# First layers of batches three and four: the seven-product block method applied a second time in four of the products, with weight sums kept in memory

## The chip, the cores and the metric

The kernel runs on one core of one Trainium2 chip. The metric is the device time of one execution in microseconds. In this text PE is TensorE (matrix products), DVE is VectorE, ACT is ScalarE, POOL is GpSimd and SP is SyncE, whose queue issues nearly all DMAs here. Every engine works through its own list of instructions in order and waits on semaphores for the others.

## What is computed

Attention with a mask by cluster (queries and keys see each other where their nearest centroids agree), for 4 batches, 8 heads, 768 positions and head size 64, and on its output a feed-forward block:

```python
attn = softmax(where(mask, q @ k.T / 8, -1e9)) @ v      # (4, 8, 768, 64)
x = attn.transpose(0, 2, 1, 3).reshape(3072, 512)
h = x @ w_in                                            # 512 x 2048
g = h * (1.0 / (1.0 + np.exp(-1.702 * h)))
out = g @ w_out                                         # 2048 x 512
```

All of it is fp32. Only the feed-forward block, and in it the first product with w_in, is touched by the change.

## The kernel before

**Stages.** First the attention of all four batches runs (to about 400 us); x of batch 0 stays on the chip, x of the later ones is kept in DRAM (`kept`) and loaded before its batch. Then the four batches of the feed-forward block follow, b = 0 to 3: a first layer (`first7` in batch 0, `first7_psum` later) and a second layer (`second49`, called for k = 0 to 6).

**Block method.** Both layers use Winograd's form of Strassen's method: a product of 2 x 2 blocks by 7 products instead of 8, with sums of blocks before and after. The first layer uses it once. The output is features by tokens; the 2048 features are two rows of FB = 8 blocks of 128, the 768 tokens two halves of HALF = 384, the inner dimension 512 two columns of two chunks of 128. For each f of 8, the seven products give G[:, f] and G[:, f+8], each with two halves h. One product has 2 matmuls of the program (c = 0, 1), 128 x 128 weights and 384 columns of x, so a first layer has 8 x 14 = 112; the profile shows two records for each matmul. The second layer uses the method twice: seven outer products (k, in the order 1, 2, 3, 6, 5, 7, 4), each of seven inner ones with 4 matmuls of QT = 192 columns, so 196 matmuls.

**Sums of weights, first layer.** `sums_w` makes for each block f the sums S2, S1, S4 on POOL, two blocks ahead, into pool `wq` (2 buffers); in batch 0 also S3, written over its place in w_in and kept there.

**Sums of x.** `sums_x` makes on DVE the tiles T2, T3, T4 (with T1 in place of an x tile) in the last steps of the second layer before.

**`first7_psum`** runs per f the products in the order 1 and 7 (w_in blocks), S2, S1, S3, S4, and w_in's (1,1). Three PSUM banks of the pool `ps_b` (6 banks) are used per f; a bank is accumulated into again after ACT (`nc.scalar.copy`) or DVE (`add`) has read it. ACT ends each quarter of G with gelu (`finish`). `after7(f)` makes on DVE one difference of G's quarters and, for f of 4 and more, the four sums `sums_t(0, f - 4)` that the second layer's k = 0 will need (M6, M5, M7, M4 there).

**`second49(k)`** runs its inner products in the order 1, 2, 6, 5, 7, 3, 4. The first goes to bank x and is copied by ACT (y11, L951); the third (6) accumulates into x. Products 6, 5 and 3 need sums of w_out's blocks (`W`, tile Wz, three thirds of 256 KB, two buffers), loaded from `kept_w` by `load_sums(k + 2)`, which SP issues after the second49 that frees the buffer. Through `extra`, the second layer's own sums, the output stores and the sums of x are spread between DVE's other work. The weights of k = 2, 3, 4 are Z_of[4], Z_of[2], Z_of[1], sums of w_out made once in batch 0; they stay on the chip. The results go to Y tiles (sums on POOL, or on DVE in the first and last batch for two of them).

**What sets the order.** Nothing is reordered by a planner (`manual_schedule`): the order on each engine is that in which the program issues its instructions. After each first layer SP has the eight loads of x for the next batch; output stores of a batch are issued at k = 4 (one of four) and in the next first layer (three, `do(pend, 1)`, one per f).

## Time and profile before

| what | value |
|---|---|
| median of 3 executions | 895.45 us (894.76 to 896.04) |
| the profiled execution | 895.92 us |
| its span, first to last instruction | 894.1 us |
| PE busy | 883.0 us (99%) |
| DVE, ACT, POOL busy | 678.4, 385.6, 482.0 us |
| a first layer of batches 1 to 3 on PE | 72.24 us |
| a second layer on PE | 63.77 us |
| DVE busy in batch 1's first layer (478.5 to 550.75 us) | 27.75 us |
| DVE busy in batch 1's second layer (550.75 to 614.5 us) | 58.03 us |
| DMA moved in all | 78.98 MB |

Times within the span count from its first instruction. A line of the timeline gives start, length, engine, source line, operation, output from inputs with their shapes, and the number of merged instructions; in brackets is the idle time before it and what ended it. A line number can be that of a helper (L598 is every sum of `sums`, L845 every `add`). A line of the table of stretches gives from:to, length, busy time and number of instructions for each engine, the granted clock of PE, the busy share of the DMA engines and GB/s.

### The profile page before, as it was taken

What the parts mean: (1) busy time and instruction counts of PE and PEld (TensorE: products, weight loads), DVE (VectorE), ACT (ScalarE), POOL (GpSimd) and SP (SyncE); (2) the same over time, 40 slices, a digit from 0 to 9 for tenths busy, and PEclk for the clock granted to TensorE, in tenths of its full rate; (3) what the DMA queues carried; (4) which work ended last, traced back from release to release, by engine and by line L of the source; (5) the groups of instructions that cost most, each with busy time, mean ns of one, the idle gap of its engine ahead of it and who ended that gap; (6) DMA issues with size and microseconds to landing.
All of it is one profiled execution on the core that took longest, in us unless ns stands there. A gap on an engine that the chain in (4) does not pass through costs nothing.

```text
span 894.1 us, 17678 instructions
## 1 busy us (share of the span) xinstructions
PE 883.0 (99%) x6720; PEld 581.9 (65%) x6720; DVE 678.4 (76%) x1097; ACT 385.6 (43%) x867; POOL 482.0 (54%) x459
## 2 busy tenths in 40 slices
PE   8999999999999999999999999999999999999997
PEld 3444444444454445557997557997556998556996
DVE  3999989999889997998896335796335797325795
ACT  3577776777677774322112333112333112333111
POOL 5899999998999998694220222233232133220130
PEclk9999999999999999999999999999999999999999
DMA  9576566666665210026213102322202223200224
GB/s 176 117 132 115 104 120 123 151 132 138 133 140 127 86 44 19 0 107 229 89 60 119 35 1 71 104 68 102 46 1 71 83 66 118 53 1 0 72 72 110
DMA packets 176334, 78.98 MB, mean 88 GB/s; under 512 B 152824, under 2 KB 159472, under 8 KB 176240
## 3 DMA queue, kind: packets, MB, share of 16 engines
q1 hardware_dynamic: 175984, 77.63, 35.8%
q8 instruction: 55, 0.90, 0.4%
q14 instruction: 39, 0.32, 0.1%
q10 hardware_dynamic: 256, 0.13, 0.1%
HBM read 61.03 MB, written 16.70 MB: 87 GB/s over the span
## 4 chain that ended last, share of the span: by engine, by line
PE 94%; DVE 4%; issue 1%; DMA 1%; ACT 0%; SPq 0%; ACTq 0%; DVEq 0%
PE b L941 25%; PE b L889 24%; PE s L472 14%; PE o L537 14%; PE b L854 8%; PE s L495 3%; PE m L554 3%; DVE G L598 2%; PE m L348 1%; DVE E L598 1%; DMA in<-in_k_dram 1%; DVE Tx L598 0%; PE o L296 0%; DVE G L845 0%; DVE y L845 0%
## 5 line engine op out<-in xcount | busy, mean ns | idle before, releaser
L521 POOL TENSOR_TENSOR sum<-sum,A 128x384 f32<-128x384 f32 x252 | 266.0, 1092 | 24.9 <-ACT A L503 16.4
L503 ACT ACTIVATE A<-s 128x768 f32<-128x768 f32 x192 | 146.1, 808 | 90.5 <-PE s L495 71.6
L845 DVE TENSOR_TENSOR G<-b,G 128x384 f32<-128x384 f32 x128 | 69.5, 556 | 142.0 <-PE b L889 135.7
L598 POOL TENSOR_TENSOR Y<-y,Y 128x768 f32<-128x768 f32 x24 | 58.1, 2435 | 165.8 <-DVE y L845 141.9
L472 PE MATMUL s<-T,T 64*64 64x384 f32 x1536 | 143.0, 487 | 0.7 <-ACT A L503 0.7
L537 PE MATMUL o<-A,inv 64*64 64x384 f32 x1536 | 141.4, 483 | 0.0
L598 POOL TENSOR_TENSOR W<-w_in 128x256 f32<-128x256 f32 x32 | 23.6, 736 | 184.8 <-PE b L889 175.0
L598 DVE TENSOR_TENSOR G<-G 128x768 f32<-128x768 f32 (+1 forms) x92 | 105.5, 1171 | 0.0
L472 PEld LDWEIGHTS s<-T,T 64*64 64x64 f32 x1536 | 55.1, 132 | 69.9 <-ACT A L503 36.4
L537 PEld LDWEIGHTS o<-A,inv 64*64 64x64 f32 x1536 | 58.9, 133 | 38.0 <-issue 32.8
L889 PE MATMUL b<-x,W 128*128 128x384 f32 x192 | 69.8, 486 | 0.0
L889 PE MATMUL b<-Tx,w_in 128*128 128x384 f32 x192 | 69.8, 486 | 0.0
L889 PE MATMUL b<-x,w_in 128*128 128x384 f32 x192 | 65.8, 486 | 0.0
L897 ACT ACTIVATE G<-G 128x384 f32<-128x384 f32 x72 | 37.7, 524 | 52.1 <-DVE G L845 52.1
L941 PE MATMUL b<-G,w_out 128*128 128x192 f32 x320 | 55.9, 326 | 0.0
L941 PEld LDWEIGHTS b<-G,w_out 128*128 128x128 f32 x320 | 52.7, 190 | 1.1
L889 PEld LDWEIGHTS b<-x,W 128*128 128x128 f32 x192 | 36.5, 190 | 25.4
L889 PEld LDWEIGHTS b<-Tx,w_in 128*128 128x128 f32 x192 | 36.5, 190 | 25.4
L889 PEld LDWEIGHTS b<-x,w_in 128*128 128x128 f32 x192 | 36.4, 190 | 24.6
L941 PE MATMUL b<-E,Wz 128*128 128x192 f32 x288 | 50.5, 327 | 0.1
L941 PEld LDWEIGHTS b<-E,Wz 128*128 128x128 f32 x288 | 47.3, 190 | 0.6 <-DVE E L598 0.4
L495 PE MATMUL s<-rows,rows 64*64 64x384 bf16 x720 | 45.6, 323 | 0.0
(182 smaller groups left out, 1518.2 us busy)
## 6 DMA issues: line engine op xcount, KB each, us to landing
Wz<-kept_w SPq DMA_DIRECT2D x78, 256.0 KB
raw<-in_moe_w_in_dram SPq DMA_DIRECT2D x16, 512.0 KB
raw<-in_moe_w_out_dram SPq DMA_DIRECT2D x16, 512.0 KB
inv<-in_v_dram SPq DMA_DIRECT2D x16, 384.0 KB
in<-in_q_dram SPq DMA_DIRECT2D x60, 96.0 KB
in<-in_k_dram SPq DMA_DIRECT2D x60, 96.0 KB
kept<-x SPq DMA_DIRECT2D x24, 192.0 KB
x<-kept SPq DMA_DIRECT2D x24, 192.0 KB
```

The source lines that it names most:

```text
L472: nc.tensor.matmul(out=ps[c:c + D, a, 0:HALF], lhsT=T[p, 1][rows, kt * P + c:kt * P + c + D], rhs=T[p, 0][rows, h * HALF:(h + 1) * HALF], ...
L495: nc.tensor.matmul(out=s_of[u][c:c + D, a, :], lhsT=rows_of[1, p % 2][rows, kt * P + c:kt * P + c + D], rhs=rows_of[0, p % 2][rows, h * HA ...
L503: nc.scalar.activation(out=A_of[u], in_=s_of.pop(u), func=AF.Exp, scale=SCALE)
L521: nc.gpsimd.tensor_tensor(out=sum_of[g][:, a], in0=(A_of[u - 1] if kt == 1 else sum_of[g])[:, a], in1=A_of[u][:, a], op=ALU.add)
L537: nc.tensor.matmul(out=o_of[g][a * D:(a + 1) * D, r, 0:HALF], lhsT=v_in[p][rows, a, kt, :], rhs=A[rows, a, :], start=(kt == 0), stop=(kt = ...
L554: nc.tensor.matmul(out=ps[a * D:(a + 1) * D, 0:HALF], lhsT=twos, rhs=sm[:, a, :], start=(i == 0), stop=(i == len(parts) - 1))
L598: engine.tensor_tensor(out=o, in0=a, in1=b, op=(ALU.add if op == "+" else ALU.subtract))
L845: nc.vector.tensor_tensor(out=o, in0=p, in1=a, op=ALU.add)
L854: nc.tensor.matmul(out=ps[:, 0:HALF], lhsT=a[:, c], rhs=x(c), start=(c == 0), stop=(c == 1))
L889: nc.tensor.matmul(out=ps, lhsT=a[:, c], rhs=x(c), start=start and c == 0, stop=(c == 1), skip_group_check=True)
L897: nc.scalar.activation(out=g, in_=g if ps is None else ps, func=AF.Gelu_apprx_sigmoid, scale=2.0)
L941: nc.tensor.matmul(out=ps, lhsT=A[n][:, f], rhs=M[n][:, f], start=start and f == 0, stop=(f == FQ - 1), skip_group_check=True)
```

## The change

- **Batch 0.** After the first layer the three Z tiles are also written to DRAM (`kept_z`, 3 x 1 MB), and after every later first layer they are loaded back, because batches 1 to 3 use their place for first-layer weights in the meantime. The POOL sums of batch 1's first two blocks are made after k = 4 of the second layer (`sums_w1`), no longer in the first layer.
- **Batch 1.** The first layer takes its blocks in the order 0, 4, 1, 5, 2, 6, 3, 7. When a pair (j, j + 4) is done, `inner_w` makes on DVE eight sums of 256 columns, the sums of weights that the second application of the method needs, and SP stores 1.5 MB to DRAM (`kept_i`).
- **Batches 2 and 3.** `first49` replaces the eight calls of `first7_psum`, and no first-layer sums are made on POOL. It works on four pairs j. Products 1, 6 and 7 (`whole`) stay as they were, 384 columns wide, in the two banks of `ps_m`; the other four are each done by seven inner products (`inner`) of 192 columns: 28 matmuls of the program per j in six banks of `ps_b`. Its 16 sums of x are made on DVE at its start. Results are put together by ACT copies, `add` from PSUM, and sums in place (`add_y5`, `close`); gelu takes a quarter of G for both blocks of a pair (768 columns). The weights of a pair are loaded from `kept_i` (`load_inner`): those of j = 0 and 1 after k = 4 of the second layer before, the later ones inside.

The diff, cut to its core:

```diff
...
     kept_w = spill.tile([7, 3, P, FQ, P], FP32, name="kept_w")
+    kept_z = spill.tile([3, P, FB, DN], FP32, name="kept_z")
+    kept_i = spill.tile([FQ, P, 24, P], FP32, name="kept_i")
+    tq = acc_p.tile([P, 2, QT], FP32, name="tq")
+    Zb = {i: z.rearrange("p f (x n) -> p (f x) n", n=P)
+          for i, z in Z_of.items()}
     def Bz(row, col, f):
...
+    TURN = [f + m * FQ for f in range(FQ) for m in range(2)]
+    def sums_w1(n):
+        if n >= FB:
+            return
+        f = TURN[n]
+        S = Zb[1 + n // 2 % 2][:, n % 2 * 6:n % 2 * 6 + 6].rearrange(
+            "p (i c) n -> p i c n", c=2)
+        w_of[FB + f] = {1: S[:, 0], 2: S[:, 1], 3: A_in(1, 0, f), 4: S[:, 2],
+                        0: S}
+        S = w_of[FB + f]
+        A11, A12, A22 = A_in(0, 0, f), A_in(0, 1, f), A_in(1, 1, f)
+        sums(nc.gpsimd, ((S[2], A22, "-", S[3]), (S[1], S[2], "+", A11),
+                         (S[4], A12, "-", S[2])))
+    def inner_w(j, S):
+        st = Zb[4]
+        def of_s(m, c):
+            return S[m][:, 0:3:2, c]
+        def of_w(m, c):
+            at = (j + m * FQ) * P
+            return w_in[:, 2 + c, :].rearrange("p (r x) -> p r x", r=2)[
+                :, :, at:at + P]
+        for n, (a, s3) in enumerate(((of_s, st[:, 0:2]),
+                                     (of_w, of_w(1, 0)))):
+            s2, s1, s4 = (st[:, i:i + 2] for i in range(2 + 6 * n, 8 + 6 * n, 2))
+            sums(nc.vector, ((s3, a(0, 0), "-", a(1, 0)),
+                             (s2, a(1, 1), "-", s3),
+                             (s1, s2, "+", a(0, 0)),
+                             (s4, a(0, 1), "-", s2)))
+        for at, x in ((slice(0, 14), st[:, 0:14]),
+                      (slice(14, 20), S[0].rearrange("p i c n -> p (i c) n")),
+                      (slice(20, 22), S[1][:, 1]),
+                      (slice(22, 24), S[1][:, 0:3:2, 1])):
+            nc.sync.dma_start(out=kept_i[j, :, at], in_=x)
+    def load_inner(j, parts=(0, 1)):
+        if j < FQ:
+            for n in parts:
+                o = (Zb[1 + j % 2], Zb[4][:, j % 2 * 8:j % 2 * 8 + 8])[n]
+                nc.sync.dma_start(
+                    out=o, in_=kept_i[j, :, (slice(0, 16), slice(16, 24))[n]])
+    Gq = G.rearrange("p f h (q t) -> p (f h q) t", t=QT)
+    SETS = ((2, 5), (3, 4))
+    def first49(X, T):
+        b = {o: {(c, q): x[:, q * QT:(q + 1) * QT]
+                 for c in range(2) for q in range(2)
+                 for x in ((X[1, 0, c], T[1, c], X[1, 1, c], T[4, c])[n],)}
+             for n, o in enumerate((2, 5, 3, 4))}
...
+        M = {}
+        for o in b:
+            M[o] = {1: b[o][0, 0], 2: b[o][1, 0], 3: b[o][1, 1],
+                    7: b[o][0, 1], **{n: rooms.pop(0) for n in (6, 5, 4)}}
+        for todo in ((2, 5), (3, 4)):
+            for n, one, op, two in ((7, 3, "-", 7), (6, 7, "+", 1),
+                                    (5, 3, "-", 6)):
+                for o in todo:
+                    sums(nc.vector, ((M[o][n], M[o][one], op, M[o][two]),))
+        for o in b:
+            sums(nc.vector, ((M[o][4], M[o][2], "-", M[o][6]),))
...
+        def quarter(j, r, h):
+            at = r * FB + j
+            return G[:, at:at + FQ + 1:FQ, h]
+        def halves(ps):
+            return ps[:, 0:HALF].rearrange("p (o t) -> p o t", t=QT)
+        def gelu(j, r, h):
+            g = quarter(j, r, h)
+            nc.scalar.activation(out=g, in_=g, func=AF.Gelu_apprx_sigmoid,
+                                 scale=2.0)
+        def whole(j, n):
+            if n == 1:
+                whole_of[j] = bank(), bank()
+            for m in range(2):
+                f = j + m * FQ
+                at = j % 2 * 8 + m * 4
+                a = {1: A_in(0, 0, f), 6: Zb[4][:, at:at + 2],
+                     7: A_in(1, 0, f)}[n]
+                x = {1: lambda c: X[0, 0, c], 6: lambda c: T[2, c],
+                     7: lambda c: T[3, c]}[n]
+                for c in range(2):
+                    nc.tensor.matmul(out=whole_of[j][m][:, 0:HALF],
+                                     lhsT=a[:, c], rhs=x(c),
+                                     start=n == 1 and c == 0, stop=c == 1,
+                                     skip_group_check=True)
+        whole_of, inner_of = {}, {}
+        def add_whole(j, r, h):
+            for m in range(2):
+                g = quarter(j, r, h)[:, m]
+                add(g, whole_of[j][m][:, 0:HALF], g)
+        def keep_whole(j):
+            y = ep.tile([P, 2, HALF], FP32, name="y")
+            for m in range(2):
+                nc.scalar.copy(y[:, m], whole_of[j][m][:, 0:HALF])
+            return y
+        def inner(j, n):
+            K, L = Zb[1 + j % 2], Zb[4][:, j % 2 * 8:j % 2 * 8 + 8]
+            if n == 2:
+                inner_of[j] = {k: [ps_b.tile([P, 512], FP32, name="b")
+                                   for _ in range(2)] for k in "zxv"}
+            ps = inner_of[j][{2: "z", 5: "v", 3: "v"}.get(n, "x")]
+            def a(o):
+                row, col, i, at = {2: (0, 1, 1, 8), 5: (0, 0, 0, 0),
+                                   3: (0, 0, 0, 1), 4: (1, 1, 1, 9)}[o]
+                if i:
...
+            for i, pair in enumerate(SETS):
+                for h, o in enumerate(pair):
+                    nc.tensor.matmul(out=ps[i][:, h * QT:(h + 1) * QT],
+                                     lhsT=a(o), rhs=M[o][n],
+                                     start=n in (1, 2, 5) and h == 0,
+                                     stop=True,
+                                     skip_group_check=True)
+            m, q, copied = {1: (0, 0, 1), 2: (0, 0, 0), 6: (0, 1, 1),
+                            5: (1, 1, 1), 3: (0, 1, 0), 7: (1, 1, 0),
+                            4: (1, 0, 1)}[n]
+            if n == 2:
+                return
+            for i in range(2):
+                o = part(j, i, m, q)
+                if copied:
+                    nc.scalar.copy(o, halves(ps[i]))
+                else:
+                    add(o, halves(ps[i]), o)
+            if n == 1:
+                for i in range(2):
+                    o = part(j, i, 0, 0)
+                    add(o, halves(inner_of[j]["z"][i]), o)
+        def add_y5(j):
+            add(quarter(j, 0, 1), quarter(j, 1, 1), quarter(j, 0, 1))
+        def close(j):
+            sums(nc.vector, ((quarter(j, 0, 1), quarter(j, 1, 1), "-",
+                              quarter(j, 0, 1)),))
+            start_t(j)
+        end = FQ - 1
+        for j in range(FQ):
+            if j == 0:
+                whole(0, 1)
+                inner(0, 2)
+                p1 = keep_whole(0)
+                whole(0, 6)
+                inner(0, 1)
+                u2 = keep_whole(0)
+                whole(0, 7)
+            else:
+                inner(j, 2)
+                inner(j, 1)
+                gelu(j - 1, 0, 0)
+                if j > 1:
+                    whole(j - 1, 6)
+                    add_whole(j - 1, 0, 1)
+                load_inner(j + 1, (1,))
+            inner(j, 5)
+            if j < end:
+                inner(j, 6)
+            if j:
+                if j > 1:
+                    whole(j - 1, 7)
+                gelu(j - 1, 0, 1)
+                add_whole(j - 1, 1, 1)
+                add_whole(j - 1, 1, 0)
+            if j == end:
+                inner(j, 6)
+            inner(j, 3)
+            if j:
+                gelu(j - 1, 1, 1)
+                gelu(j - 1, 1, 0)
+            if j == end:
+                whole(j, 1)
+                p1 = keep_whole(j)
+            inner(j, 7)
+            if j == end:
+                whole(j, 6)
+                u2 = keep_whole(j)
+            elif j:
+                whole(j, 1)
+            inner(j, 4)
+            if j == end:
+                whole(j, 7)
+            load_inner(j + 2, (0,))
+            if j == end:
+                break
+            add_y5(j)
+            if j:
+                add_whole(j, 0, 0)
+                close(j - 1)
+            else:
+                for h, o in enumerate((p1, u2)):
+                    g = quarter(0, 0, h)
+                    add(g, o, g)
+                do(pend, 3)
+        g = quarter(end, 0, 0)
+        add(g, p1, g)
+        gelu(end, 0, 0)
+        close(end - 1)
+        add_y5(end)
+        g = quarter(end, 0, 1)
+        add(g, u2, g)
+        gelu(end, 0, 1)
+        start_t(end)
+        add_whole(end, 1, 1)
+        gelu(end, 1, 1)
+        add_whole(end, 1, 0)
+        gelu(end, 1, 0)
+        sums(nc.vector, ((quarter(end, 0, 1), quarter(end, 1, 1), "-",
+                          quarter(end, 0, 1)),))
     def second49(k, extra, last):
...
+        if b == 1:
+            done = None
+            for n, f in enumerate(TURN):
+                made_w = w_of[FB + f][0]
+                first7_psum(b, f, *XT)
+                if n % 2 == 0 and done:
+                    inner_w(*done)
+                sums_w1(n + 2)
+                if n:
+                    after7(TURN[n - 1])
+                if n % 2 == 0:
+                    one = made_w
+                else:
+                    done = f - FQ, (one, made_w)
+                do(pend, 2)
+            after7(FB - 1)
+            inner_w(*done)
+        if b > 1:
+            first49(*XT)
+        for f in range(FB if b == 0 else 0):
+            first7(b, f, *XT)
+            if f + 2 < FB:
+                sums_w(f + 2)
             if f:
                 after7(f - 1)
-            do(pend, 1)
             if b == 0 and f < 3:
                 for n in range(3 * f, min(3 * f + 3, FB)):
                     sums_z((nc.gpsimd, nc.vector, nc.vector)[n % 3], n)
@@ -1080,7 +1359,13 @@
                     keep_w(k, spare_y())
                 if 5 <= f < 7:
                     load_sums(f - 5)
-        after7(FB - 1)
+        if b == 0:
+            after7(FB - 1)
+        for n, i in enumerate((4, 2, 1)):
+            if b == 0:
+                nc.sync.dma_start(out=kept_z[n], in_=Z_of[i])
+            else:
+                nc.sync.dma_start(out=Z_of[i], in_=kept_z[n])
         if b < B - 1:
             for h in range(2):
                 for hp in range(HP):
...
+            if k == 4 and b == 0:
+                sums_w1(0)
+                sums_w1(1)
+            if k == 4 and 0 < b < B - 1:
+                load_inner(0)
+                load_inner(1)
             if k < 5:
                 load_sums(k + 2, b == 0 and k > 2)
             elif b < B - 1:
```

More of the change, by code (lines that the diff above doesn't have):

```diff
@@ L923, in after7, with start_t @@
         if f >= FQ:
-            for _ in sums_t(0, slice(f - FQ, f - FQ + 1)):
-                pass
+            start_t(f - FQ)
+    def start_t(f):
+        for _ in sums_t(0, slice(f, f + 1)):
+            pass
+    TURN = [f + m * FQ for f in range(FQ) for m in range(2)]
[11 more added lines that the diff above has]
+                         (S[4], A12, "-", S[2])))
@@ new lines, in load_inner, with part @@
+    def load_inner(j, parts=(0, 1)):
[11 more added lines that the diff above has]
+             for n, o in enumerate((2, 5, 3, 4))}
+        rooms = [tq[:, i] for i in range(2)]
+        for _ in range(2):
+            r = wq.tile([P, 3, 2, P], FP32, name="W").rearrange(
+                "p i c n -> p (i c n)").rearrange("p (n t) -> p n t", t=QT)
+            rooms += [r[:, i] for i in range(4)]
+        rooms += [ep.tile([P, QT], FP32, name="p5") for _ in range(2)]
+        M = {}
[9 more added lines that the diff above has]
+            sums(nc.vector, ((M[o][4], M[o][2], "-", M[o][6]),))
+        def part(j, i, m, q):
+            one = ((j + m * FQ) * 2 + i) * 2 + q
+            step = FB * 4 + (2, -2)[i]
+            return Gq[:, one:one + step + 1:step]
+        def quarter(j, r, h):
[42 more added lines that the diff above has]
+                if i:
+                    one, two = (A_in(row, col, j + m * FQ) for m in range(2))
+                    known = {1: one[:, 0], 2: one[:, 1], 4: two[:, 1],
+                             7: two[:, 0]}
+                    s2 = at
+                elif o == 5:
+                    known = {1: K[:, 14], 2: K[:, 15], 4: L[:, 6], 7: K[:, 0]}
+                    s2 = 2
+                else:
+                    known = {1: L[:, 2], 2: L[:, 3], 4: L[:, 7], 7: K[:, 1]}
+                    s2 = 3
+                known.update({6: K[:, s2], 5: K[:, s2 + 2], 3: K[:, s2 + 4]})
+                return known[n]
+            for i, pair in enumerate(SETS):
[98 more added lines that the diff above has]
+                          quarter(end, 0, 1)),))
@@ L1065, in fast @@
     for b in range(B):
-        for f in range(FB):
-            (first7_psum if b else first7)(b, f, *XT)
-            sums_w(b * FB + f + 2)
+        if b == 1:
[21 more added lines that the diff above has]
+                sums_w(f + 2)
             if f:
                 after7(f - 1)
-            do(pend, 1)
             if b == 0 and f < 3:
@@ L1082, in fast @@
                     load_sums(f - 5)
-        after7(FB - 1)
+        if b == 0:
[3 more added lines that the diff above has]
+                nc.sync.dma_start(out=kept_z[n], in_=Z_of[i])
+            else:
+                nc.sync.dma_start(out=Z_of[i], in_=kept_z[n])
         if b < B - 1:
```

## The prediction

> **What bounds the kernel now.** I read first the engines' busy time and the chain that ended last on the page, then that chain in order of time from 519 us on.

> ```profile
> span 894.1 us, 17678 instructions
> PE 883.0 (99%) x6720; PEld 581.9 (65%) x6720; DVE 678.4 (76%) x1097; ACT 385.6 (43%) x867; POOL 482.0 (54%) x459
> PE 94%; DVE 4%; issue 1%; DMA 1%; ACT 0%; SPq 0%; ACTq 0%; DVEq 0%
> ```
> ```profile
> 550.91 63.78 PE b L941 x392
> 614.70 72.24 PE b L889 x224
> 686.94 63.77 PE b L941 x392
> 750.71 72.24 PE b L889 x224
> ```
> TensorE sets the time. A first layer (L889) and a second layer (L941) follow each other without a gap. Each matmul of the program shows as two records, so a 384-column matmul costs 72.24/112 = 0.645 us and a 192-column one 63.77/196 = 0.3254 us, half as much. Fewer columns pay fully, but no wait is hidden any more: what keeps PE waiting is added to the end.

> Then I read VectorE and the DMA queue around the end of a second layer (here batch 1).

> ```profile
> 600.53 2.30 DVE L598 TENSOR_TENSOR G<-G 128x768 f32<-128x768 f32 x1
> 602.87 2.45 DVE L598 TENSOR_TENSOR E<-G 128x768 f32<-128x768 f32 x1
> 605.24 0.34 DVE L845 TENSOR_TENSOR y<-y,p 128x192 f32<-128x192 f32 x1
> 605.51 0.94 DVE L598 TENSOR_TENSOR E<-G,E 128x768 f32<-128x768 f32 x1
> ```
> ```profile
> 599.27 1.91 SPq L1034 DMA_DIRECT2D out_dram<-Tx  x4
> 601.28 13.42 SPq L796 DMA_DIRECT2D Wz<-kept_w  x9
> ```
> ```profile
> 599.65 4.85 POOL L598 TENSOR_TENSOR Y<-y,Y 128x768 f32<-128x768 f32 x2 [5.44 <-DVE y L845]
> ```
> VectorE is full from 567 to 615 us, and an operation of 0.94 us takes 2.3 to 2.45 us while POOL works. The output stores stand on SP ahead of the weights for k=6, which are issued at 601.3 us; PE needs them 2.6 us after k=6 starts (605.43), at 608.0.

> In batch 0 VectorE has no room left at all: k=5 should reach its third product 2.60 us after its start, at 462.54, and reaches it at 462.84, when the sum Tx is ready.

> ```profile
> 459.94 2.76 PE L941 MATMUL b<-G,w_out 128*128 128x192 f32 x16
> 462.84 1.54 PE L941 MATMUL b<-Tx,Wz 128*128 128x192 f32 x8
> ```

> [...] The page agrees that there is one queue (77.63 MB in q1), so a load waits for all bytes ahead of it. [...]

> ```profile
> 560.50:561.00 0.50, 0.50 (x5) 0.50 (x4) 0.00 (x0) 0.00 (x0) 0.00 (x0) 1.00 1.01 385
> 561.00:561.50 0.50, 0.50 (x5) 0.50 (x4) 0.00 (x0) 0.01 (x1) 0.00 (x0) 1.00 1.04 397
> ```
> (last column GB/s, before it the share of the DMA engines; their weights come in 2 KB rows). I take 385 GB/s, and 330 for the x loads, whose rows are 1.5 KB (321 GB/s at a share of 0.98). [...] The trace has 0.35 (N=192), 0.55 (384) and 0.95 us (768)[...].

> **The change, part by part.**

> *Matmuls.* In batches 2 and 3, four of seven products become 7/8 of their columns: 64 x 0.645 = 41.28 us go, 112 x 0.3254 = 36.44 come, the other 48 x 0.645 = 30.96 stay. That is -4.84 us a batch, **-9.7** in all. PE's bare time for such a first layer is 67.4 us. The pieces have the shape of the second layer's matmuls, weight load each time, so I take their cost from there. If each took its weight load's 190 ns per record, the gain would be gone: 112 x 2 x 0.19 = 42.6.

> *Waits inside such a first layer.* I laid the program's order out on each engine, t from the start of the batch, with: 0.2 us from a matmul's end to its reader, ACT copy of 384 columns 0.48 (the next may begin after 0.4), gelu of 768 about 0.85 (0.52 for 384, scaled with the 0.808 of the 768-wide exponent), VectorE add from PSUM 0.56 (next after 0.48), 768-wide sum 0.95 (0.87), 192-wide 0.35 (0.33).
> - The 16 sums of x at the start take 5.3 us behind at most 2 us of older work; PE needs the first twelve at 10.3 us. Hidden, and about 4 us are to spare.
> - j=0: whole(0,7) overwrites the bank that keep_whole reads. Those copies are queued behind the two of inner(0,1), which end at 8.4; the first is done at 8.85 and PE, ready at 7.76, goes on at 9.0: **1.2**. inner(0,4) then waits **0.2** for the add of inner(0,7).
> - j=1: whole(1,1) takes the two banks of whole(0,.). VectorE frees them after y5, two sums, three stores' transposes (6 x 0.51), two adds and four adds: 9.0 us after j=1 starts; PE is there at 7.8: **1.3**.
> - The weights L of j=2 are issued behind twelve output DMAs (0.48 us each on SP, from 4.6 us on), land some 14.2 us after j=1 starts and are wanted at 13.65: **0.6**.
> - j=2 and j=3: adds come in time by 0.3 to 1 us.
> - The end: after inner(3,4) VectorE has a 768 sum, close (768 + 4 x 192), y5, another 768, 4 x 192, and four adds from PSUM, 8.1 us, and only then can ACT do the last gelu. The copy y11 of the second layer's first product stands behind that gelu on ACT, and the third product accumulates into the bank that it reads. From inner(3,4)'s first half: 0.7 (copy) + 8.1 + 0.9 + 0.35 + hand-offs 0.3 = 10.3; PE has 5.85 us of work (0.65 + 2.58 + 2.6). **4.4**.
> Together 7.7 a batch, **+15.4**. SP, POOL and VectorE have no other bound here: VectorE is busy some 11 of 16.9 us per j.

> *Batch 0.* Six POOL sums move from the first layer to k=5 of the second, 6 x 0.73 = 4.4 us. VectorE loses about 0.6 of that (4.75 us for two sums of 0.95 above), 2.6 us, with no idle time until the end and PE already waiting for it: **+2.4** (0 if POOL fits a gap, 4.4 at most). Writing kept_z (3.15 MB) and the x loads stand ahead of Wz for k=2: 5.75 MB from 412 us at some 370 GB/s, so Wz lands near 430 us, wanted at 435.

> *Batch 1, first layer.* The 32 sums of inner_w are 256 wide, [...]at most the 0.55 of 384[...]. VectorE is busy 27.75 us of that layer's 72.25: hidden. In iteration 2, sums_w1 must wait for inner_w (done 2.9 us after that block) and for the store of its S (1.31 MB, to 7.8); its first sum is ready at 8.6, PE wants it at 11.6. Nothing; without that cover up to 2 us.

> *Batch 1, k=2.* SP now has ahead of Wz for k=2: the last kept_i (1.57 MB, from 4.9 us after the layer's end), three kept_z (3.15) and x (1.57). Data flows from 5.8: 4.72/0.385 + 1.57/0.33 = 17.0, so at 22.8 Wz begins, and its first third is there at 23.8. PE wants it at 18.2 + 2.6 = 20.8: **+3.0** (+4.4 if all three thirds are waited for). Batches 2 and 3 have no kept_i there and make it.

> *k=6 of batches 1 and 2.* load_inner(0) and (1), 3.15 MB, are put between the stores and Wz for k=6: 8.2 us. Before, Wz was all there at 605.4 (its 0.79 MB, 2 us, at the end), first third 1.4 earlier; needed 608.0, room 4.0. In batch 2 it was there at 742.2, first third 740.8, needed 743.9: room 3.1. So **+5.0** in batch 2, and 4.2 in batch 1, less 1.5 there, since the stop at k=2 lets VectorE's lag shrink and the stores go sooner: **+2.7**.

> *Nothing:* the POOL sums of batches 2 and 3 (48 x 0.73) are gone, hidden before; the kept_z loads of batches 2 and 3.

> Sum: -9.7 + 15.4 + 2.4 + 3.0 + 5.0 + 2.7 = **+18.8**. The profiled execution took 895.92 us (894.1 span and 1.8 around it), giving 914.7; the median lies 0.47 lower: **914.3 us**.

> **The rivals.**
> - *Transfers come in time* [...]: no DMA wait, -10.7 and -1.2 for L: 902.4. For it: the copies are large and PE's earlier stops give them time; against: one queue, in order.
> - *Transfers come later still*: all thirds waited for (3 x 1.4), 330 GB/s (3 x 1.3), batch 1's stores not sooner (1.5): +9.6, 923.9.
> - *The pieces cost more on PE*, 190 ns a record: the change does not save what it says, +9.7 to +12: about 925.
> - *Ending faster: engines do not keep the written order.* If a planner let y11 go ahead of the gelus, the u2 copies ahead of others and Wz ahead of the inner loads, the waits made by order alone would go: 2 x (1.2 + 4.4), 3.0, 2.7 and 5.0, together 21.9: 892.3. It decides as soon as all waits stay under 9.7 us. Against it: the order written is that of the trace on VectorE and SP (stores at 599.3 ahead of Wz).

> **Numbers.** My sum 0.50, transfers in time 0.17, later 0.12, dearer pieces 0.06, order loosened 0.15. The last gives faster by over 0.2% (1.8 us, what a measurement of this kernel can tell from none) 0.13 and same 0.02; from an early-transfer case with shorter waits comes 0.02 more same: 0.13, 0.04, 0.83. The range goes from 898 (the loosened case left out, 0.15) to 926 (about 0.05).

> **What would show it.** PE idle of some 4 us at the third product of the second layers of batches 2 and 3, waiting for ACT's y11, itself behind a gelu; 1 us stops at whole(0,7) and whole(1,1); Wz waits at k=2 of batch 1 and k=6 of batches 1 and 2; in batch 0 waits for VectorE at k=5 and k=6; PE time of L889's successors 67.4 us a batch. I am wrong if those second layers start without a stop, or Wz lands by its use.

## The result, and the profile after

The changed kernel takes 933.66 us (median of 5 executions, 932.04 to 934.20), the kernel before, run beside it, 896.04 us: a ratio of 1.0413 with a 95% interval of 1.0387 to 1.0439. (The ratio compares fast runs; one execution of the kernel before took 905.46 us, far from its other four.) The forecast was 914.3 us, in a range of 898 to 926; the direction was right and the size half of the true one: +37.6 us in place of +18.8.

The head of the page and the shares of the chain that ended last, in the kernel after:

```profile
span 930.2 us, 18202 instructions
PE 888.1 (95%) x6912; PEld 616.4 (66%) x6912; DVE 728.9 (78%) x1217; ACT 393.7 (42%) x867; POOL 448.8 (48%) x411
PE 78%; DVE 13%; DMA 5%; issue 2%; SPq 1%; ACT 1%; POOL 0%; DVEq 0%; ACTq 0%
```

The chain was PE for 94% and is PE for 78% now: DVE and DMA stand in it where PE waits. Note also that PE is busy 5.1 us *longer* than before, although by the forecast it has 9.7 us less to do. PE's waits after 400 us, in us in total, number of times and longest one:

```profile
PE b L1201 <- DMA Wz<-kept_w: 14.1, 3, 5.6
PE b L1201 <- ACT Y L1211: 8.1, 2, 4.0
PE b L1085 <- DMA Z<-kept_i: 2.6, 2, 1.3
PE b L1201 <- DVE Tx L598: 2.3, 1, 2.3
PE b L1201 <- DVE E L598: 2.1, 2, 1.5
PE m L1040 <- ACT y L1055: 1.9, 2, 1.0
PE m L1040 <- DVE G L850: 1.2, 2, 0.6
```

Each of these seven waits stands in the prediction, with its place; together they are 32.3 us (the prediction has 28.5). By stage, in us from the first matmul of one stage to that of the next:

| stage | before | after | difference | forecast |
|---|---|---|---|---|
| second layer, batch 0 | 64.4 | 69.0 | +4.6 | +2.4 |
| first layer, batch 1 | 72.2 | 72.2 | 0 | 0 |
| second layer, batch 1 | 63.8 | 76.7 | +12.9 | +5.7 |
| first layer, batch 2 (new) | 72.2 | 71.3 | -1.0 | -1.5 |
| second layer, batch 2 | 63.8 | 78.5 | +14.7 | +9.4 |
| first layer, batch 3 (new) | 72.2 | 71.2 | -1.0 | -1.5 |
| second layer, batch 3 | 64.0 | 70.0 | +6.0 | +4.4 |

(What the forecast calls the wait at the end of the new first layer falls into the second layer behind it.) The second layers of batches 1 to 3 lose more than their waits. The products behind the five long stops, from the timeline of PE in the kernel after; in brackets the idle time before each:

```profile
580.75 4.23 PE L1201 MATMUL b<-E,Wz 128*128 128x192 f32 x16 [4.63 <-DMA Wz<-kept_w]
622.68 5.43 PE L1201 MATMUL b<-E,Wz 128*128 128x192 f32 x16 [3.91 <-DMA Wz<-kept_w]
709.93 4.50 PE L1201 MATMUL b<-E,Wz 128*128 128x192 f32 x16 [4.04 <-ACT Y L1211]
772.00 5.46 PE L1201 MATMUL b<-E,Wz 128*128 128x192 f32 x16 [5.57 <-DMA Wz<-kept_w]
859.55 4.55 PE L1201 MATMUL b<-E,Wz 128*128 128x192 f32 x16 [4.05 <-ACT Y L1211]
```

Sixteen such records take 2.76 us elsewhere in this trace. Here they take 4.2 to 5.5. The table of stretches around the first of these stops shows why; its third column from the right is PE's granted clock:

```profile
575.90:580.70 4.80, 0.22 (x2) 0.00 (x0) 4.77 (x5) 0.00 (x0) 1.16 (x1) 0.94 1.06 387
580.70:582.10 1.40, 1.35 (x4) 1.39 (x5) 0.17 (x1) 0.00 (x0) 0.00 (x0) 0.50 1.06 391
582.10:583.50 1.40, 1.40 (x6) 1.40 (x6) 0.00 (x0) 0.00 (x0) 0.00 (x0) 0.50 0.41 151
583.50:585.00 1.50, 1.50 (x11) 1.50 (x10) 0.00 (x0) 0.32 (x1) 0.00 (x0) 0.97 0.00 0
```

Towards the end of this stop, at 580.2 us, the clock falls to half, and PE goes on at half speed until 583.6 us: 4 and 6 records in stretches that hold 9 at full clock.

### The profile page after: what moved, and what is told of

It reads as the page before. It is cut to its first block, busy times and chain, and to the rows that moved or that the text cites. A ratio compares the mean times of both kernels' runs of the same rounds, so it can differ in the third digit from the quotient of the medians.

```text
span 930.2 us, 18202 instructions
## 1 busy us (share of the span) xinstructions
PE 888.1 (95%) x6912; PEld 616.4 (66%) x6912; DVE 728.9 (78%) x1217; ACT 393.7 (42%) x867; POOL 448.8 (48%) x411
## 4 chain that ended last, share of the span: by engine, by line
PE 78%; DVE 13%; DMA 5%; issue 2%; SPq 1%; ACT 1%; POOL 0%; DVEq 0%; ACTq 0%
PE b L1201 19%; PE s L472 12%; PE o L537 12%; PE b L859 8%; PE b L894 8%; PE b L1085 6%; PE m L1040 6%; DVE G L598 3%; PE s L495 3%; PE m L554 3%; DMA Wz<-kept_w 2%; DVE G L850 2%; DVE E L598 2%; PE m L348 1%; DMA x<-kept 1%
## 5 line engine op out<-in xcount | busy, mean ns | idle before, releaser
L598 POOL TENSOR_TENSOR Y<-y,Y 128x768 f32<-128x768 f32 x24 | 57.5, 2410 | 353.8 <-DVE y L850 320.2
L598 DVE TENSOR_TENSOR G<-G 128x768 f32<-128x768 f32 (+1 forms) x84 | 102.7, 1248 | 0.1
L1201 PE MATMUL b<-E,Wz 128*128 128x192 f32 x288 | 60.9, 372 | 24.3 <-DMA Wz<-kept_w 14.1
L1201 PEld LDWEIGHTS b<-E,Wz 128*128 128x128 f32 x288 | 56.5, 221 | 26.5 <-issue 16.7
L1098 ACT COPY G<-b 128x384 f32<-128x384 f32 x64 | 30.4, 478 | 62.1 <-PE b L1085 62.1
L495 PEld LDWEIGHTS <-rows 64*64 64x64 bf16 x720 | 23.1, 107 | 33.1 <-issue 32.1
L1201 PE MATMUL b<-G,Wz 128*128 128x192 f32 x224 | 41.0, 326 | 0.0
L1217 ACT COPY y<-b 128x192 f32<-128x192 f32 x24 | 7.6, 319 | 76.5 <-PE b L1201 76.5
L1201 PE MATMUL b<-G,Z 128*128 128x192 f32 x224 | 39.0, 326 | 0.0
L521 POOL TENSOR_TENSOR sum<-A 128x384 f32<-128x384 f32 x32 | 37.2, 1184 | 0.0
L1201 PEld LDWEIGHTS b<-G,Wz 128*128 128x128 f32 x224 | 37.2, 190 | 0.0
L1201 PEld LDWEIGHTS b<-G,Z 128*128 128x128 f32 x224 | 36.8, 190 | 0.0
```

What stands on the lines that cost most here:

```text
L495: nc.tensor.matmul(out=s_of[u][c:c + D, a, :], lhsT=rows_of[1, p % 2][rows, kt * P + c:kt * P + c + D], rhs=rows_of[0, p % 2][rows, h * HA ...
L521: nc.gpsimd.tensor_tensor(out=sum_of[g][:, a], in0=(A_of[u - 1] if kt == 1 else sum_of[g])[:, a], in1=A_of[u][:, a], op=ALU.add)
L598: engine.tensor_tensor(out=o, in0=a, in1=b, op=(ALU.add if op == "+" else ALU.subtract))
L1201: nc.tensor.matmul(out=ps, lhsT=A[n][:, f], rhs=M[n][:, f], start=start and f == 0, stop=(f == FQ - 1), skip_group_check=True)
```

## Theories and experiments

**Theory A**: a stop costs its own length and then the time that PE runs at half clock. From the end of a stop to the next outer or first-layer product PE should take 6.5 us; behind the five stops (at 580.75, 622.68, 709.93, 772.00 and 859.55 us) it takes 1.5, 2.7, 1.7, 3.1 and 1.9 us more, 10.9 in all. **Theory B**: what follows a stop is slow because the things waited for come in pieces (three thirds of Wz, four sums), and the clock is a companion. Both take the causes of the stops from the prediction; the experiments test these too. A gain is given against the changed kernel's +37.6 us over the kernel before, each run against the kernel before on its own chip. By the intervals of the two ratios, a gain under some 3 us is not clear of noise.

**PE kept busy during the stops** (`e1_busy`). `fill(n)` is called ahead of the third product, with n = 20 and 16 at k=2 and k=6 of batch 1, 16 and 24 at k=0 and k=6 of batch 2, and 16 at k=0 of batch 3; nothing else changes:

```diff
+    def fill(n):
+        if n:
+            ps = ps_b.tile([P, 512], FP32, name="b")
+            for _ in range(n):
+                nc.tensor.matmul(
+                    out=ps, lhsT=ident_h,
+                    rhs=ident_h[:, None, :].broadcast_to((P, 4, P)),
+                    start=True, stop=True)
...
         extra(0)
+        fill(FILL.get((at_b[0], k), 0))
         product(x, 6, False)
```

> Ahead of the third product of five second layers (k=2 and k=6 of batch 1, k=0 and k=6 of batch 2, k=0 of batch 3) PE gets 16 to 24 matmuls of 128 x 512 bf16 that nobody reads, so that it is busy for most of the stop; what it waits for stays as it is. Theory A (half clock): after a stop of 4 us or more PE runs at half its granted clock for some microseconds, which costs 10.9 us over the five stops (1.5 + 2.7 + 1.7 + 3.1 + 1.9); kept busy it starts again at full clock: 933.7 - 10.9 = 922.8 us, clock 0.99 or more, the stops' ends where they were. Theory B (aftermath): the slow part after a stop is a wait for further pieces (the other thirds of Wz, the next sums); then nothing changes, 933 to 935 us.

Measured: 923.69 us against 895.93, +27.8, ratio 1.0302 (1.0281 to 1.0323): a gain of 9.9 us, at a mean clock of 0.997. The first of the five products behind a stop, in the timeline of PE:

```profile
576.67 4.48 PE L1194 MATMUL b<-ident_h 128*128 128x512 bf16 x20
582.24 2.84 PE L1213 MATMUL b<-E,Wz 128*128 128x192 f32 x16 [1.09 <-DMA Wz<-kept_w]
```

It still begins 5.6 us late (4.48 busy, 1.09 idle), but its 16 records take 2.84 us. Work that nobody reads made the kernel 9.9 us faster. That is theory A; pieces that arrive late would be as late here. The 9.9 us are net of a loss elsewhere: in the new first layers the waits for kept_i grew from 2.6 to 4.8 us in the profiled execution, and behind one of them, of 2.5 us, the clock was half for 3.4 us.

**Wz of k=6 ahead of the inner weights** (`e2_wz`):

```diff
+            if k < 5:
+                load_sums(k + 2, b == 0 and k > 2)
             if k == 4 and 0 < b < B - 1:
                 load_inner(0)
                 load_inner(1)
             if k < 5:
-                load_sums(k + 2, b == 0 and k > 2)
+                pass
```

> The weights Wz of k=6 are issued ahead of the inner weights of j=0 and 1 (one swap on SP's queue). If those 3.15 MB ahead of Wz are the cause of the stops at k=6 of batches 1 and 2, their idle time goes, 3.9 + 5.6 us, and by theory A also the slow part behind them, 2.7 + 3.1: 933.7 - 15.3 = 918.4 us. By theory B with a slow part that has another cause, 924.2 us. If the output stores ahead of Wz hold it, no change.

Measured: 917.16 against 895.93, +21.2, ratio 1.0237 (1.0218 to 1.0256): a gain of 16.4 us. One swap of SP's order takes both stops and their half-clock time away; among PE's waits for Wz only that of k=2 in batch 1 is left (4.3 us).

**The end of the new first layer put behind the second layer's first products** (`e3_tail`). `rest` holds the six steps that are taken out here, in their order; `start_t` moves up:

```diff
         close(end - 1)
+        start_t(end)
         add_y5(end)
         g = quarter(end, 0, 1)
         add(g, u2, g)
-        gelu(end, 0, 1)
-        start_t(end)
-        add_whole(end, 1, 1)
-        gelu(end, 1, 1)
-        add_whole(end, 1, 0)
-        gelu(end, 1, 0)
-        sums(nc.vector, ...)
+        return rest
...
         add(y11, z, y11)
+        if rest:
+            rest.pop()()
         extra(0)
```

> At the end of the new first layer the last three gelus, the four adds and the last difference are put behind the first copy y11 and the first add of the second layer, and the eight sums that k=0 needs are made before y5. If y11 behind the gelus is the cause of the stops at k=0 of batches 2 and 3, their idle time goes, 4.0 + 4.1 us, and by theory A the slow part, 1.7 + 1.9: 933.7 - 11.7 = 922.0 us; by theory B 925.6 us. If the sums M6 of VectorE stand right behind, 1 to 2 us of each stop stay.

Measured: 924.92 against 895.93, +29.0, ratio 1.0319 (1.0301 to 1.0338): a gain of 8.6 us, 3 less than expected. The cause of the stop was right, for the copy y11 is done early now and the product behind it starts without a wait. But the gelus now stand ahead of the next copy, y12, and the fifth product of the layer waits for that; in the timeline of PE of this run:

```profile
705.31 2.76 PE L1206 MATMUL b<-E,Wz 128*128 128x192 f32 x16
709.88 1.54 PE L1206 MATMUL b<-Y,w_out 128*128 128x192 f32 x8 [1.80 <-ACT Y L1224]
```

That is 1.8 us in batch 2 and, by the same wait, 2.3 us in batch 3, where the clock was half for 3.4 us afterwards. I had not foreseen these stops. Their 4.1 us of idle time, with the half clock, are enough for the 3 us that are missing.

**x of batch 2 behind Wz of k=2** (`e4_x_later`): in batch 1 the eight loads are issued after `load_sums(2)`.

```diff
-        if b < B - 1:
+        def load_x():
             for h in range(2):
...
+        if b < B - 1:
+            if b not in (1,):
+                load_x()
             made = sums_x(b + 1)
...
                 load_sums(k + 2, b == 0 and k > 2)
+                if k == 0 and b in (1,):
+                    load_x()
```

> In batch 1 the eight loads of x are issued after Wz of k=2 instead of ahead of it. If bytes ahead of Wz are the cause of the stop at k=2, 1.57 MB fewer bring Wz in some 4.8 us earlier: the stop of 4.8 us and by theory A its slow part of 1.5 go, 927.4 us; by theory B 928.9 us.

Measured: 926.44 against 895.93, +30.5, ratio 1.0342 (1.0324 to 1.0361): a gain of 7.1 us. PE's wait for Wz at k=2 of batch 1, 4.63 us in the changed kernel, is 0.64 us in this trace: the 1.57 MB of x ahead of Wz in the one queue are the cause of this stop.

**A stop by itself in the kernel before** (`b1_stop_short`, `b2_stop_long`, `b3_stop_2us`): ten, sixteen and eight ACT copies ahead of y11, at k=0 of batches 1 to 3 (`first` is set in batch 0).

```diff
         product(x, 1, True)
+        if i == 1 and not first:
+            for _ in range(10):
+                nc.scalar.copy(idle_a, w_in[:, 0, 0:HALF])
         nc.scalar.copy(y11, x)
```

> The kernel before, with ten ACT copies of 384 columns that nobody reads put ahead of y11 at k=0 of batches 1, 2 and 3, so that the third product of these three second layers waits some 2.3 us for ACT (10 x 0.42 us + 0.65 after the layer's start, less 2.6). Theory A (half clock only after long stops): three stops of 2.3 us at full clock afterwards, 895.5 + 7 = 902 us, clock as before. If any stop halves the clock, another 1.7 us or more each, 907 us or more.

> The same with sixteen copies, so that each of the three stops is some 4.8 us long. Theory A: 895.5 + 3 x 4.8 and for each stop 1.7 to 3.1 us at half clock: 915 to 919 us. Theory B (PE goes on at full clock, the loss in the changed kernel came from its weights and sums): 909 to 910 us.

> The kernel before with eight idle ACT copies instead of ten or sixteen. Ten gave stops of 3.50 us and sixteen 6.75 us, 0.54 us for each copy, so eight give 2.4 us. [...] 895.5 + 3 x 2.4 = 902.7 us in every execution, granted clock 0.997 as before. If the clock is halved by chance after shorter stops too: 904 to 909 us, and executions that differ by more than 2 us.

The stops came out at 3.50, 6.75 and 2.40 us (for the first two 2.3 and 4.8 had been expected, so their forecast times cannot be compared as they stand). Measured, against 895.46, 895.46 and 896.04: 912.39 (ratio 1.0186, 1.0169 to 1.0203), 923.36 (1.0313, 1.0295 to 1.0330) and 907.46 us (1.0131, 1.0114 to 1.0148). The idle time of three stops is 10.5, 20.3 and 7.2 us; the kernels lose 16.9, 27.9 and 11.4 us. So there are 6.4, 7.6 and 4.2 us more than idle time, with nothing changed in weights, sums or DMA: theory A again, and theory B cannot explain it. These stops are PE's only waits after 400 us in the three traces. In the last of them half clock came after stops of 2.4 us too; three such stops at full clock would have given 902.7 us. The middle and the last of the three equal stops in the profiled execution of `b1_stop_short`:

```profile
695.90 2.87 PE L942 MATMUL b<-E,Wz 128*128 128x192 f32 x16 [3.50 <-ACT Y L955]
```
```profile
835.61 5.49 PE L942 MATMUL b<-E,Wz 128*128 128x192 f32 x16 [3.50 <-ACT Y L955]
```

The same stop is once followed by full clock and once by half. In `b3_stop_2us` half clock followed two of the three stops of 2.4 us. What the traces show of the difference is in the last section.

**POOL's sums** (`e5_pool`, `e9_hold`). `e9_hold` puts a one-element sum that reads G of batch 1 ahead of the POOL sums of blocks two and three; `e5_pool` does that and also makes those of the first two blocks in batch 0's first layer.

```diff
+        if n in (2, 3):
+            one = G[:, TURN[n - 2], 0, 0:1]
+            sums(nc.gpsimd, ((S[:, 0, 0, 0:1], one, "+", one),))
         w_of[FB + f] = ...
```

> The POOL sums of batch 1's first two blocks are made in batch 0's first layer again, in tiles of wq, and those of the next two are held on POOL until batch 1's first layer runs. If POOL's twelve sums in batch 0's second layer are what makes VectorE late there, its stops at k=5 and k=6 (2.3 + 0.6 + 1.5 us) and some 0.5 us of smaller ones go: 933.7 - 4.6 = 929.1 us. If the stores of kept_z or the loads are the cause, no change.

> Of the change in batch 0 only one thing is mended: the POOL sums of batch 1's blocks two and three are held until batch 1's first layer runs (a one-element sum ahead of each that reads G of batch 1). Six of twelve POOL sums stay in batch 0's second layer. If POOL running ahead was the part that the prediction missed (4.9 us lost there instead of 2.4), about half of the 5.9 us that the mend of all twelve brought comes back: 933.7 - 2.5 to 3.5 = 930.2 to 931.2 us. If the first six alone hold VectorE up, 933 us or more.

Measured: `e5_pool` 927.76 against 895.46, +32.3, ratio 1.0350 (1.0333 to 1.0367), a gain of 5.3 us, and no wait for DVE is left in batch 0; `e9_hold` 931.02 against 896.04, +35.0, ratio 1.0396 (1.0379 to 1.0413), a gain of 2.6 us. The second gain alone is not clear of noise; the traces say more. Of PE's waits for DVE in batch 0's second layer, 4.4 us in the changed kernel, `e9_hold` has 2.3 left, all at k=5 (in that execution the clock was half for 3.4 us behind it, which gives DVE time as well). The changed kernel had not six POOL sums in batch 0's second layer but twelve; here the first and the last of them, in the timeline of POOL:

```profile
457.46 1.44 POOL L598 TENSOR_TENSOR Z<-w_in 128x256 f32<-128x256 f32 x1
...
470.76 1.43 POOL L598 TENSOR_TENSOR Z<-w_in,Z 128x256 f32<-128x256 f32 x1
```

The second six belong to batch 1's first layer in the program, but nothing on POOL or in memory holds them back, and POOL is through with them more than 10 us before that layer begins (482.9).

**All mends together** (`e7_all`): e2, e4 and e5; the end of the layer as in e3, but in pieces, with the gelu that k=1 needs behind y12 and the others behind y22; and inside the new first layer:

```diff
+                u2 = keep_whole(0)
                 inner(0, 1)
-                u2 = keep_whole(0)
...
+            if j == 0:
+                load_inner(2, (1,))
...
+                add_whole(0, 1, 1)
+                add_whole(0, 1, 0)
                 do(pend, 3)
```

> All mends together: Wz of k=6 ahead of the inner weights, x of batch 2 behind Wz of k=2, the end of the new first layer put behind the first products of the second in three pieces, the POOL sums as in batch 0's first layer of before; and inside the new first layer the copies u2 ahead of those of inner(0,1), the adds that free the banks of j=0 and the weights L of j=2 ahead of the stores. If the matmuls saved are worth 9.7 us once no stop is left, 895.5 - 9.7 + some 3 us of short stops = 889 us. If another wait stands right behind those taken away (VectorE's sums, the stores), 893 to 900 us.

Measured: 886.78 against 895.46, ratio 0.9895 (0.9879 to 0.9912): 8.7 us faster than the kernel before and 47 us faster than the changed one, with the same arithmetic. In the table of stretches these are its new first layer and second layer of batch 2:

```profile
614.90:682.65 67.75, 67.75 (x321) 54.49 (x321) 41.67 (x91) 28.83 (x53) 0.00 (x0) 1.00 0.29 86
682.65:746.35 63.70, 63.70 (x394) 63.70 (x393) 60.46 (x80) 13.03 (x37) 20.60 (x8) 1.00 0.54 191
```

PE has no idle time in either, and the new first layer takes 67.75 us in place of 72.24. One wait of PE is left after 400 us:

```profile
PE b L1220 <- DMA Wz<-kept_w: 1.3, 1, 1.3
```

**The Z loads later too** (`e8_z_later`): in batch 1, `load_z(1)` and `load_z(2)` are issued beside `load_x()`, behind Wz of k=2.

> All mends, and in batch 1 the loads of Z_of[2] and Z_of[1] (2.1 MB, wanted at k=3 and k=4) also behind Wz of k=2. The one stop that is left in the trace of all mends, 1.3 us at k=2 of batch 1, goes: 886.8 - 1.3 = 885.5 us. If the later Z loads come too late for k=3, as slow as before or slower, 887 us or more.

Measured: 887.23 against 896.04, ratio 0.9896 (0.9880 to 0.9913). The trace shows no wait of PE any more after 400 us, and the second layer of batch 1 takes 63.7 us in place of 65.3. But the time cannot be told from that of `e7_all`: 1.3 us is less than the interval of the ratio (1.5 us to each side), and in this profiled execution the attention ahead took 1.5 us longer, with nothing changed in it (the first second layer starts at 414.31 us, in `e7_all` at 412.86).

## Why the prediction was wrong

Point by point, by its own steps:

- **Matmuls, -9.7**: right. Without stops the new first layer takes 67.75 us (bare time forecast: 67.4), so the two save 9.0 us against 72.24 each. The pieces cost what the second layer's matmuls cost, within 0.35 us a layer; the rival of dearer pieces is out.
- **Waits inside the new first layer, 3.3 a batch**: right in place, but the size came out by luck: 0.95, 0.58 and 1.34 us in batch 2 for the forecast's 1.2, 1.3 and 0.6, with errors that cancel. They are gone in `e7_all`, whose edits inside this layer are aimed at them.
- **The end, 4.4**: right, 4.04 and 4.05 us, by the copy behind the gelus (`e3_tail`, `e7_all`).
- **First layer of batch 1, 0**: right, 72.2 us before and after. The 32 sums of `inner_w` took 0.42 us each on DVE, 13.5 us in all, less than the 0.55 us that the prediction has as the most.
- **k=2 of batch 1, 3.0, and k=6, 2.7 and 5.0**: right in cause (`e4_x_later`, `e2_wz`), small in size: 4.6, 3.9 and 5.6 us. At k=2 the data began to flow when forecast, but nearly stood still around 565 us (82 GB/s in that microsecond), where SP waited for the store of kept_i to end before it issued the Z loads. At k=6 of batch 1 the stores went out only 0.4 us sooner, not 1.5. The rival of later transfers thus has a part in it: 14.1 us for the three, where my sum has 10.7 and that rival 20.3.
- **Batch 0, 2.4**: mis-sized by half. The step said "Six POOL sums move from the first layer to k=5 of the second"; twelve ran in that second layer, since nothing held POOL back from the six that belong to the next stage. 4.6 us were lost (69.0 for 64.4). With six alone (`e9_hold`) the waits for DVE are 2.3 us, close to what the step had for six.
- **The step that failed** is the one that the whole sum rests on: "no wait is hidden any more: what keeps PE waiting is added to the end". Each stop was priced at its own length. In the runs PE's clock also fell to half, for 3.4 or 6.8 us at a time, at stops of 2.3 us and more: in the changed kernel it was 0.5 from 580.2 to 583.6, 621.1 to 627.9, 709.9 to 713.3, 771.3 to 778.1 and 860.1 to 863.5 us. The second layers of batches 1 to 3 show PE busy for 68.2, 68.9 and 65.9 us with the work of 63.8, 63.8 and 64.0: 11.4 us that no step had. 10.5 of them are the clock: half of the time that PE was busy while it was halved. `e1_busy` gives 9.9 back with the stops left in place, and three stops put into the kernel before cost 4 to 8 us more than they last.

So, of the 36.1 us that the span grew: -9.0 saved, +32.3 idle (28.5 forecast), +11.4 in the second layers, nearly all of it half clock (none forecast), and +1.3 around the three short waits in each new first layer, where PE's records take longer (68.40 us a layer, in `e7_all` 67.75). Without the half clock the kernel would, by this estimate (933.66 less 10.5), have ended near 923 us, inside the range; `e1_busy` came out at 923.69. Two small slips in the prediction's sums change nothing: the 5.75 MB ahead of and with Wz in batch 0 are 5.5, and 914.3 - 21.9 is 892.4.

A hint stood in the kernel before: it has matmuls that nobody reads at its start and at the start of its attention (`keep_busy`).

The rival of loosened order is out: the waits that the prediction named went away when the written order was changed (with a hold for POOL's sums), and in `e8_z_later` none of them is left.

## What to carry to other kernels

On PE, busy for 99% here, a stop cost its length and, where the clock fell, half of PE's busy time in the 3.4 or 6.8 us at half clock, 10.5 us over five stops; of the stops of 2.2 to 2.6 us seven in twelve did it here, so look at every stop of that length, and try PE at work through one that cannot be avoided (`e1_busy`: 9.9 us). A saving on the bounding engine is worth what the other queues' order lets through: here one swap on SP was worth 16.4 us, more than the whole saving of 9. When work moves, ask for each engine that does it what holds it back; where nothing does, it runs early, and collides where nobody planned it.

## What the runs showed that was not expected

```profile
690.99:694.40 3.41, 1.41 (x9) 1.12 (x7) 2.71 (x8) 3.22 (x7) 0.15 (x1) 1.00 0.00 0
830.94:834.35 3.41, 1.17 (x8) 0.87 (x6) 1.81 (x7) 3.19 (x8) 0.00 (x0) 1.00 0.00 0
```

The first, with PE busy for 1.41 us (the first figure behind the length), was followed by full clock, the second, with 1.17, by half clock from 834.35 us on. The first of these stops lies across two slots, with PE busy for 1.41 us in one and, from 695.90 us on, for 1.9 us in the next. Counted from the span's start, the slots lie differently in these executions: one begins at 3.31 us in the changed kernel, at 1.50 in `b1_stop_short`, 2.78 in `b2_stop_long` and 1.13 in `b3_stop_2us`. This was read from the traces afterwards; no run was made to test it.

- The fall can come after PE is at work again: in the stop at 855.5 us PE started at 859.55, and the clock fell at 860.1, where the slot from 856.6 us, with PE busy for 0.51 us, ended.
- In batch 0's second layer POOL and DVE were both slower beside each other: the POOL sums of 128x256, 0.73 us at 518 us, took up to 1.44 beside DVE's sums, and a DVE sum of 128x768 (E from G and Tx), 0.95 us in the kernel before, took 1.48 beside POOL's (at 465.24 us).
